# A light attention with a top-80 mixture of experts: one projection product per token group, earlier output clearing, and a listed order

## The chip, the cores and the metric

The kernel runs on one core of a Trainium2 chip. The metric is the device time of one execution in microseconds (us); lower is better. Of the kernel before there are three timed runs and one profiled execution.

## The reference

The input x has 8 x 3584 = 28672 tokens of 192 numbers, and each token has 8 heads with 7 raw weights. The first part replaces each token by a weighted sum over itself and the six tokens before it, with a softmax of the seven weights in each head:

```
w = exp(weight_gen - max);  w = w / (sum(w) + 1e-9)
out = einsum('bshk,bskhg->bshg', w, x_unf)
```

The second part is a mixture of 8 experts on the result. Each token goes to the expert of its largest gate logit; each expert keeps at most its 80 tokens of highest gate probability; every other row of the output is zero:

```
logits = x @ w_gate;  expert_idx = argmax(logits);  gate_w = softmax(logits)[expert_idx]
for e: keep = the (at most) 80 tokens of e with the largest gate_w
       out[keep] = gate_w[keep] * (relu(x[keep] @ w1[e]) @ w2[e])
```

So all tokens need logits, and only 640 rows need the experts and are stored with values other than zero.

## The kernel before, in words

**Stage A, logits of all tokens** (`gates`). The 128 partitions hold 128 runs of 224 consecutive tokens. x comes in 28 loads of 8 token positions (L385), transposed, from the host's layout: 96 partitions hold six of the eight positions, and the 32 further partitions hold the other two in three pieces, so a load is a full 128 x 1536 tile of 768 KB. TensorE projects each load on the gate, head by head, into a PSUM bank `pt`: four matmuls with 96 rows and 384 columns (L439) for the first six positions, then twelve with 32 rows and 128 columns (L444), three per output piece, for the other two. Only one `pt` bank exists. ScalarE copies it out (L448), TensorE transposes it into the PSUM tile `y` (L482), and for each of 14 chunks (8, 9, 9 and eleven times 18 positions) the seven-tap products with the softmax weights are formed head by head: five heads on VectorE, three on GpSimd (L547; in the last two chunks four on GpSimd, `NPOOL`). TensorE sums the products by transposing matmuls into `acc` (L563, seven per head), ScalarE copies, and TensorE turns the chunk back (`bt`, L577). The softmax of the raw weights runs three chunks ahead (L408 to L415), and `gate` turns the logits of a few chunks into gate probabilities.

**Stage B, selection.** For every expert a threshold is found: the top values per lane (`MAX` at L920), two rounds of counting (L871, L876), then the chosen tokens are numbered, their rows are gathered (L979), ranked exactly, and the totals are checked.

**Stage C, experts.** For the gathered rows the attention is done again in full (L992 to L1040, "attend"), then come the two matrix products of each expert (L1295 and L1299 up, L1319 down; "FFN"; expert 0 and 1 with 128 columns and the others with 80), and the scaled rows are stored to their places (L1334).

**Zeros of the output.** 28 transfers of 768 KB from a cleared tile `zt` (L1588) write the zeros. 22 go out during and after the loads of x; the last six (`late_zeros`) take a second tile `zt2` that is cleared only when the gathers have been issued.

**Order.** A `Plan` collects all operations with costs and dependences, and a list scheduler with random restarts (`order`) fixes the order on every engine. Each engine then issues in this order and waits by semaphores. Transfers of x, of the raw weights, of expert weights and zeros share SyncE's queue. Buffers: 4 of x (the same ring holds w1), 6 of raw weights (the same ring holds halves of w2). `issue` puts otherwise useless matmuls ("fillers") into TensorE's idle time: 128x128 ones before the first `acc` (`spin`, L643), 128x512 ones in stage B (L1325) and among the attends (L1268, L1269), and 14 before anything else (L637).

**Start.** The gate is loaded by three DMAs from ScalarE's queue (L338, L340), because the block layout `bd` is needed on 96 and on 32 partitions; VectorE takes the differences (L359) and fills `bd` (L362). GpSimd clears `zt`, `lg`, `vt` and some small tables by memsets.

Of the kernel before, what the change touches and what calls it, by code (L numbers as in the profile page):

```python
# [9 lines left out]
F32 = mybir.dt.float32  # L10
# [21 lines left out]
NQ = 1 + DH // (P - DH)  # L32
# [4 lines left out]
NPOOL = [3] * (len(SIZES) - 2) + [4] * 2  # L37
# [6 lines left out]
XB = 4  # L44
WB = 6
# [11 lines left out]
LATE = GE[-3]  # L57
NC = C
NH = 2
# [13 lines left out]
ZT = 512  # L73
# [3 lines left out]
SEED = 9  # L77
NOISE = (0.3, 1.0, 3.0, 6.0)
WE = 2
FILL = 0.6  # L80
FILL0 = 0.9
POOLED = frozenset(['am4', 'am5', 'bad', 'gs4', 'gs6', 'gx7', 'hb', 'hbt', 'kp0', 'lad', 'ohf0', 'pr00', 'pr10', 'pr11', 'pr21', 'pr61', 'pr70', 'prc1', 'sid', 'thr', 'v11'])
ZA = 18
ZH = 22
ZS = 10
ZP = 1.5
# [5 lines left out]
class Plan:  # L92
# [4 lines left out]
    READY = {"PE": 0.6, "ACT": 2.0, "DVE": 3.3, "POOL": 2.0}  # L97
    SAME = {"PE": 0.0, "ACT": 0.1, "DVE": 0.08, "POOL": 0.06, "DMA": 0.0}

    def __init__(self):  # L100
# [14 lines left out]
        self.port = []  # L115

# [54 lines left out]
    def _run(self, pred, succ, prio, rel, fwd):  # L171
# [19 lines left out]
        for _ in range(n):  # L191
# [13 lines left out]
            if best is None:  # L205
# [4 lines left out]
                    key=lambda k: (est[k] if fwd and e == "DMA" else 0.0, prio[k], k))  # L210
# [22 lines left out]

    def order(self):
        ops = self.ops
# [98 lines left out]

def consts(tc, cp, gate):
    nc = tc.nc
    gg = cp.tile([P, 2, NQ, E], F32, name="gg")
# [18 lines left out]
    for lo, hi, qa, qb in ((0, DH, NQ - 1, NQ), (DH, P, 0, NQ - 1)):
        for t in range(2):
            gt = gg[lo:hi, t, qa:qb]
# [9 lines left out]
def gates(pl, tc, pools, xt, wgen, ident, bd, epst, zb, lg, V, VL, tie, after, clear, ZH):  # L368
# [1347 lines left out]
```

## Time and profile before

| what | value |
|---|---|
| three runs | 257.09 us median (256.98 to 257.61) |
| profiled execution, own time | 257.11 us |
| its span, first to last instruction | 255.3 us |
| TensorE busy | 233.2 us, 91% of the span |
| VectorE busy | 187.5 us, 73% |
| GpSimd busy | 183.4 us, 72% |
| ScalarE busy | 87.4 us, 34% |
| moved by DMA | 68.36 MB, mean 268 GB/s |

The span leaves 1.8 us of the profiled time outside. A busy share is a mean over stages, so the sections below go by stretches of the span: up to 27 us the ramp, to 160 us the rest of stage A, to 196 us the selection with the first attends, and then the experts. A row of the timeline reads: start, duration, engine, line, operation, output and input, and in brackets how long the engine had been idle before and what ended that.

### The profile page before, as it was taken

How to read it: one execution, taken by the hardware profiler on the slowest of the kernel's cores; microseconds unless marked ns; L12 is line 12 of the kernel's file. 1: busy time of each engine (PE TensorE's matmuls, PEld its weight loads, DVE VectorE, ACT ScalarE, POOL GpSimd, SP SyncE). 2: the span in 40 equal slices, each digit the busy share in tenths (PEclk: the TensorE clock that was granted, in tenths of full speed). 3: DMA queues.
4: the chain of work that ended last, by engine and by line, in shares of the span. 5: the costliest groups of instructions: out<-in, count | busy, mean ns of one | idle time of the engine just before them, and what ended most of it. 6: DMA issues, size and time to landing. Idle time of an engine off the chain costs nothing. (4 is left out here: it accounts for less than half of the span.)

```text
span 255.3 us, 5886 instructions
## 1 busy us (share of the span) xinstructions
PE 233.2 (91%) x2317; PEld 184.1 (72%) x2317; DVE 187.5 (73%) x377; ACT 87.4 (34%) x215; POOL 183.4 (72%) x197
## 2 busy tenths in 40 slices
PE   8689999999999999999999999559789999999970
PEld 3457668788769878976888989347337897999960
DVE  2663679679949968999996999886583549899300
ACT  2341554283336227246613452320012122232310
POOL 6597688999979997998993979437477644436320
PEclk9955999999999999999999999755665799999997
DMA  6994778999969899859999996200899789995000
GB/s 231 425 349 154 274 242 233 361 307 407 341 200 416 334 287 384 337 188 278 412 400 406 401 383 263 62 0 17 202 347 385 238 296 289 332 283 197 19 13 17
DMA packets 22642, 68.36 MB, mean 268 GB/s; under 512 B 2418, under 2 KB 2935, under 8 KB 22608
## 3 DMA queue, kind: packets, MB, share of 16 engines
q1 hardware_dynamic: 20704, 63.05, 68.2%
q0 software_dynamic: 1472, 4.85, 7.6%
q8 instruction: 20, 0.33, 0.5%
q14 instruction: 14, 0.11, 0.1%
q10 hardware_dynamic: 432, 0.01, 0.1%
HBM read 45.40 MB, written 22.59 MB: 266 GB/s over the span
## 5 line engine op out<-in xcount | busy, mean ns | idle before, releaser
L563 PE MATMUL acc<-ident,P 128*126 128x128 f32 (+1 forms) x700 | 86.5, 278 | 0.0
L547 POOL TENSOR_TENSOR P<-ysb,w 128x882 f32<-128x882 f32 (+2 forms) x44 | 76.6, 1773 | 12.5 <-ACT ysb L502 12.4
L563 PEld LDWEIGHTS acc<-ident,P 128*126 128x126 f32 (+1 forms) x700 | 77.8, 141 | 5.2 <-issue 3.6
L547 DVE TENSOR_TENSOR P<-y,w 128x882 f32<-128x882 f32 (+2 forms) x68 | 61.9, 961 | 13.3 <-ACT hs L508 12.2
L444 PEld LDWEIGHTS pt<-x,bd 32*32 32x32 f32 x672 | 17.3, 108 | 21.0 <-issue 18.1
L448 ACT ACTIVATE yt<-pt 128x512 f32<-128x512 f32 (+2 forms) x29 | 16.8, 581 | 37.9 <-PE pt L444 37.8
L409 POOL TENSOR_TENSOR w<-w,m 128x1008 f32<-128x1008 f32 (+2 forms) x14 | 24.8, 1780 | 4.9 <-DVE m L408 4.9
L444 PE MATMUL pt<-x,bd 32*32 32x128 f32 x672 | 25.3, 282 | 2.5 <-ACT yt L448 2.5
L415 POOL TENSOR_TENSOR w<-w,r 128x1008 f32<-128x1008 f32 (+2 forms) x14 | 25.2, 1816 | 2.3 <-DVE gm L614 1.2
L439 PE MATMUL pt<-x,bd 96*32 96x384 f32 x224 | 25.2, 523 | 0.0
L1319 PE MATMUL F<-w,hu 128*80 128x192 f32 (+1 forms) x128 | 22.7, 326 | 0.0
L1023 DVE TENSOR_REDUCE ao<-pr 80x96 f32<-80x672 f32 (+3 forms) x14 | 18.0, 1305 | 4.0 <-POOL pr L1019 4.0
L1319 PEld LDWEIGHTS F<-w,hu 128*80 128x80 f32 (+1 forms) x128 | 18.7, 160 | 1.1
L412 DVE TENSOR_REDUCE m<-w 128x144 f32<-128x1008 f32 (+2 forms) x14 | 14.9, 1074 | 5.3 <-ACT w L411 5.3
L482 PE MATMUL y<-ident,yt 128*128 128x128 f32 (+1 forms) x116 | 17.6, 285 | 0.8 <-ACT yt L448 0.8
L411 ACT ACTIVATE w<-w 128x1008 f32<-128x1008 f32 (+2 forms) x14 | 13.3, 948 | 11.0 <-POOL w L409 11.0
L482 PEld LDWEIGHTS y<-ident,yt 128*128 128x128 f32 (+1 forms) x116 | 13.7, 146 | 2.6 <-issue 1.3
L408 DVE TENSOR_REDUCE m<-w 128x144 f32<-128x1008 f32 (+2 forms) x14 | 14.6, 1063 | 1.2 <-DMA w<-wgen 1.1
L414 DVE RECIPROCAL r<-m 128x144 f32<-128x144 f32 (+2 forms) x14 | 13.2, 947 | 2.3 <-ACT m L413 2.2
L1019 POOL TENSOR_TENSOR pr<-gx 88x672 f32<-88x672 f32 (+2 forms) x6 | 9.8, 1647 | 6.1 <-DVE gx L998 6.0
L1299 PE MATMUL F<-ax,w 128*128 128x80 f32 x96 | 13.7, 266 | 0.0
L1334 POOL DMA_INDIRECT out<-yo,sidx x6 | 6.2, 1042 | 10.0 <-ACT yo L1332 7.2
(268 smaller groups left out, 330.1 us busy)
## 6 DMA issues: line engine op xcount, KB each, us to landing
x<-xt SPq DMA_DIRECT2D x28, 768.0 KB, 6.0
out<-zt SPq DMA_DIRECT2D x28, 768.0 KB, 10.2
w<-w2p SPq DMA_DIRECT2D x16, 384.0 KB, 6.7
w<-w1p SPq DMA_DIRECT2D x8, 768.0 KB, 7.3
w<-wgen SPq DMA_DIRECT2D x11, 504.0 KB, 6.5
w<-wgen SPq DMA_DIRECT2D x2, 252.0 KB, 5.2
w<-wgen SPq DMA_DIRECT2D x1, 224.0 KB, 2.8
gx<-wgen,tux POOLq DMA_INDIRECT x6, 5.0
```

The lines of the kernel that those rows point to most:

```text
L408: op("DVE", dve(nw), lambda: nc.vector.tensor_reduce(out=m(), in_=w(), axis=AX.X, op=ALU.max), r=[wn], w=[mn])
L409: op("POOL", pool_flat(nw), lambda: nc.gpsimd.tensor_tensor(out=w(), in0=w(), in1=bcast_last(m(), K), op=ALU.subtract), r=[mn], w=[wn])
L412: op("DVE", dve(nw), lambda: nc.vector.tensor_reduce(out=m(), in_=w(), axis=AX.X, op=ALU.add), r=[wn], w=[mn])
L415: op("POOL", pool_flat(nw), lambda: nc.gpsimd.tensor_tensor(out=w(), in0=w(), in1=bcast_last(r(), K), op=ALU.mult), r=[rn], w=[wn])
L439: o = nc.tensor.matmul(pl[f"pt{g}"][32 * c:32 * c + 32, 0:3 * P], lhsT=bd[0:DH, c % 2, NQ - 1, :], rhs=x[0:DH, 3 * c:3 * c + 3, :], start= ...
L444: o = nc.tensor.matmul(pl[f"pt{g}"][32 * c:32 * c + 32, 3 * P:4 * P], lhsT=bd[DH:P, c % 2, r, :], rhs=x[DH:P, 3 * c + r, :], start=(r == 0 ...
L448: op("ACT", act(hi - lo), lambda: nc.scalar.activation(out=pl[f"yt{g}"][:, lo:hi], in_=pl[f"pt{g}"][:, lo:hi], func=AF.Copy), r=[f"pt{g}"] ...
L482: o = nc.tensor.matmul(pl[yn][:, u - s0 + sh:v - s0 + sh, :], lhsT=src, rhs=idn, is_transpose=True, start=True, stop=True)
L547: return (nc.gpsimd if onpool else nc.vector).tensor_tensor(out=out, in0=in0, in1=in1, op=ALU.mult)
L563: o = nc.tensor.matmul(pl[an][0:M, :], lhsT=pl[f"P{c}_{i}"][:, k, 0:M], rhs=ident, is_transpose=True, start=(n == 0 and k == 0), stop=(n = ...
L1023: V_(K * G * (h1 - h0), lambda h0=h0, h1=h1: v.tensor_reduce(out=pl[sn][0:rows, h0 * G:h1 * G], in_=pl[pn][0:rows, :, h0 * G:h1 * G].rearr ...
L1319: o = nc.tensor.matmul(yp(), lhsT=hs[q]()[:, j * n:(j + 1) * n], rhs=pl[f"w2_{e}{q}"][:, j % 2 * 2 + j // 2, :], start=(q == 0 and j == 0) ...
```

## The change

1. **x on 96 partitions.** The host now lays all eight positions on 96 partitions and pads 32 partitions with zeros: a load is a 128 x 2048 tile of 1 MiB, and the projection is four matmuls with 96 rows and 512 columns (L498 of the changed kernel). The twelve 32-row matmuls are gone. `bd`, the mask and the gate lie on 96 partitions, and the gate is one DMA.
2. **Clears on ScalarE.** A helper `blank` copies from a small zero tile by ScalarE activations (L397); 14 such clears stand before the first exponential on ScalarE. Three casts per group of selection candidates (`split`) move from GpSimd to ScalarE too.
3. **Zeros.** Rows of 3 KB in place of 2 KB; all 28 transfers from one tile, marked `spare`, so that the scheduler sends them when nothing else is due; no late zeros.
4. **Banks and fillers.** The small selection products no longer use the `pt` bank but parts of two `y` tiles (`S1`, `S2`). Fillers in stage B write to `S2` (`keep_awake`, L1331, L1332); the fillers of the ramp have 512 columns.
5. **Three heads on GpSimd in all chunks.**
6. **A listed order.** A table `STARTS` of one start per operation gives the order of every engine; the scheduler is used only if the table does not fit.

```diff
-NPOOL = [3] * (len(SIZES) - 2) + [4] * 2
+NPOOL = [3] * len(SIZES)
-ZT = 512
+ZT = 768
+STARTS = """
+7l 96 5k 63 l4 83 8l gw cf 73 ia al bq dg y0 yw m5 zs w3 xa 9l go h4 hw kp i3 bi b0 iz bw jp d3 mv vm wt 8d b5 g2 1o
...
-ZH = 22
-ZS = 10
-ZP = 1.5
+ZS = 5
+ZP = 0.8
...
+        return nc.scalar.activation(out=a, in_=z, func=AF.Copy)
+    pl.op("ACT", act(n), go, w=nm)
...
-    nc.scalar.dma_start(gg[0:DH, :, NQ - 1, :], gate.rearrange("(t d) e -> d t e", d=DH))
-    for t in range(2):
-        nc.scalar.dma_start(gg[DH:P, t, 0:NQ - 1, :], gate[t * DH:(t + 1) * DH].rearrange("(r d) e -> d r e", d=P - DH))
+    gg = cp.tile([DH, 2, E], F32, name="gg")
+    nc.scalar.dma_start(gg, gate.rearrange("(t d) e -> d t e", d=DH))
...
-        new(f"x{n}", lambda: xp.tile([P, 12, P], F32, name=f"x{n}", tag="x"), "x", XB)
+        new(f"x{n}", lambda: xp.tile([P, 16, P], F32, name=f"x{n}", tag="x"), "x", XB)
...
-            if lo == 0:
-                for c in range(4):
-                    o = nc.tensor.matmul(pl[f"pt{g}"][32 * c:32 * c + 32, 0:3 * P], lhsT=bd[0:DH, c % 2, NQ - 1, :],
-                                         rhs=x[0:DH, 3 * c:3 * c + 3, :], start=True, stop=True)
-            if hi == 4 * P:
-                for r in range(NQ - 1):
-                    for c in range(4):
-                        o = nc.tensor.matmul(pl[f"pt{g}"][32 * c:32 * c + 32, 3 * P:4 * P], lhsT=bd[DH:P, c % 2, r, :],
-                                             rhs=x[DH:P, 3 * c + r, :], start=(r == 0), stop=(r == NQ - 2))
+            for c in range(4):
+                o = nc.tensor.matmul(pl[f"pt{g}"][32 * c:32 * c + 32, lo:hi], lhsT=bd[:, c % 2, :],
+                                     rhs=x[0:DH, 4 * c + lo // P:4 * c + hi // P, :], start=True, stop=True)
...
-        for _ in range(int(gap * FILL0 / 0.1067)):
-            nc.tensor.matmul(pl["warm"][:, 0:P], lhsT=zb, rhs=zb, start=True, stop=True)
+        for _ in range(int(gap * FILL0 / 0.2134)):
+            nc.tensor.matmul(pl["warm"], lhsT=zb, rhs=with_ap(zb, [[0, 4], [1, P]]), start=True, stop=True)
...
-        op("POOL", pool(n), lambda: g.tensor_copy(out=p(2), in_=c()), r=[f"cand{nm}"], w=[f"pv{nm}"])
+        op("ACT", act(n), lambda: nc.scalar.activation(out=p(2), in_=c(), func=AF.Copy), r=[f"cand{nm}"], w=[f"pv{nm}"])
...
-        bank(bn, [RC, 2])
+        bsv = lambda: pl["S1"][0:RC, 0, 2 * E + 2 * q:2 * E + 2 * q + 2]
...
-    def late_zeros():
-        op("POOL", pool(8), lambda: nc.gpsimd.memset(zt2[:, 0:8], 0.0), w=["zt2b"], dep=[sm["go"]])
-        for _ in range(ZH, NZ):
-            clear(late=True)
...
+    def keep_awake():
+        new("S2", lambda: ps_y.tile([P, 3, 512], F32, name="S2", tag="y"), "y", 2, parts=["warmy", "plc", "tfp"])
+        def fill(gap):
+            for _ in range(int(gap * FILLY / 0.2134)):
+                nc.tensor.matmul(pl["S2"][:, 0, :], lhsT=zb, rhs=with_ap(zb, [[0, 4], [1, P]]), start=True, stop=True)
...
-        def zero(i, eng=nc.sync, src=zt):
-            return eng.dma_start(ov[:, i * ZC:(i + 1) * ZC].rearrange("p (a b) -> p a b", b=ZT),
-                                 with_ap(src, [[0, ZC // ZT], [1, ZT]]))
+        def zero(i):
+            return nc.sync.dma_start(ov[:, i * ZC:(i + 1) * ZC].rearrange("p (a b) -> p a b", b=ZT),
+                                     with_ap(zt, [[0, ZC // ZT], [1, ZT]]))
...
+                    pl.spare.add(zeros[-1])
...
-    xt = np.empty((NX_, P, 2, 2, 3, P), dtype=x.dtype)
+    xt = np.zeros((NX_, P, 2, 2, 4, P), dtype=x.dtype)
```

**TensorE in the middle of stage A.** `pt` are projections, `acc` the sums of a chunk's products (seven matmuls per head), `y` the transposes. Before:

```order
L439 MATMUL pt_994<-x_809,bd 32x384 x4
L444 MATMUL pt_994<-x_809,bd 32x128 x12
L563 MATMUL acc_925<-ident,P_3_933 126x128 x7
L563 MATMUL acc_925<-ident,P_4_949 126x128 x7
L439 MATMUL pt_1040<-x_838,bd 32x384 x4
L444 MATMUL pt_1040<-x_838,bd 32x128 x12
L563 MATMUL acc_1064<-ident,P_0_1013 126x128 x7
```

In the changed kernel:

```order
L617 MATMUL acc_770<-ident,P_3_762 126x128 x7
L617 MATMUL acc_770<-ident,P_4_780 126x128 x7
L498 MATMUL pt_862<-x_718,bd 32x512 x4
L617 MATMUL acc_872<-ident,P_0_815 126x128 x7
L617 MATMUL acc_872<-ident,P_5_833 126x128 x7
L498 MATMUL pt_896<-x_740,bd 32x512 x4
```

Each projection is one group of four matmuls in place of two groups of four and twelve; what stands between two projections is the same kind of work.

**VectorE around the last product of stage A.** `P_..<-y` are products, `cand` the top eight of an expert's lanes, `ix` their places, `gm` belongs to the gate probabilities. Before:

```order
L920 MAX cand<-vt 112x8 x6
L547 TENSOR_TENSOR P_3_2348<-y_2119,w_1402 128x882
L920 MAX cand<-vt 112x8
L928 MAX_INDEX ix<-cand,vt 112x8 x6
L610 TENSOR_REDUCE gm_2391<-lg 128x18
```

In the changed kernel, from the last product on:

```order
L601 TENSOR_TENSOR P_4_1971<-y_1699,w_1193 128x882
...
L974 MAX cand<-vt 112x8
L669 RECIPROCAL gm_1939<-gm_1939 128x18
L974 MAX cand<-vt 112x8
L672 SCALAR_TENSOR_TENSOR VL<-lg,gm_1939 128x144
L974 MAX cand<-vt 112x8 x3
L982 MAX_INDEX ix<-cand,vt 112x8
L974 MAX cand<-vt 112x8
L982 MAX_INDEX ix<-cand,vt 112x8
L974 MAX cand<-vt 112x8
```

All eight `MAX` now stand behind the last product; before, seven of them stood ahead of it.

**SyncE at the end of the loads of x.** `x` are loads, `out<-zt` zeros, `w_<n>` from `w1p` and `w2p` expert weights. Before:

```order
L385 DMA x_1847<-xt 128x1536
L1588 DMA out<-zt 128x3x512
L1252 DMA w_0_1916<-w1p 128x1536
L1588 DMA out<-zt 128x3x512 x10
L1259 DMA w_10_2292<-w2p 128x768
...
L1588 DMA out<-zt_65 128x3x512 x6
L1252 DMA w_4_2875<-w1p 128x1536
```

In the changed kernel:

```order
L445 DMA x_1557<-xt 128x2048
L1303 DMA w_0_1588<-w1p 128x1536
L1310 DMA w_10_1619<-w2p 128x768
L1303 DMA w_1_1632<-w1p 128x1536
L1303 DMA w_2_1661<-w1p 128x1536
L1651 DMA out<-zt 128x2x768 x3
L1310 DMA w_11_1775<-w2p 128x768
...
L1651 DMA out<-zt 128x2x768 x10
L1303 DMA w_4_2510<-w1p 128x1536
```

Eight zeros stand ahead of the last load of x where eleven did, and the other 20 stand behind it, between the weights of the first four experts, ahead of the fifth expert's.

## Rows read from the trace of the kernel before

**Rows 1.** Page, busy time and share of the span, by engine.

```profile
PE 233.2 (91%) x2317; PEld 184.1 (72%) x2317; DVE 187.5 (73%) x377; ACT 87.4 (34%) x215; POOL 183.4 (72%) x197
```

**Rows 2.** Windows: length, busy time (instructions) per engine, PEclk, DMA share, GB/s.

```profile
27.00:160.00 133.00, 132.96 (x1615) 107.47 (x1612) 116.48 (x162) 59.83 (x131) 120.57 (x89) 1.00 0.90 325
160.00:196.00 36.00, 26.82 (x181) 16.91 (x180) 25.00 (x121) 6.40 (x25) 19.76 (x42) 0.59 0.52 161
...
0.00:120.00 120.00, 115.67 (x1374) 85.52 (x1375) 91.75 (x119) 50.89 (x102) 104.17 (x100) 0.94 0.85 301
124.00:140.00 16.00, 15.96 (x178) 13.57 (x177) 13.94 (x17) 4.99 (x15) 12.42 (x10) 1.00 1.04 406
12.00:27.00 15.00, 14.24 (x121) 9.14 (x119) 7.62 (x14) 4.86 (x12) 11.14 (x19) 0.54 0.73 270
```

**Rows 3.** Timeline of TensorE's matmuls, 30 to 33 us.

```profile
30.04 0.85 PE L439 MATMUL pt<-x,bd 96*32 96x384 f32 x8
30.82 0.86 PE L444 MATMUL pt<-x,bd 32*32 32x128 f32 x24
31.61 1.64 PE L563 MATMUL acc<-ident,P 128*126 128x128 f32 x13
```

**Rows 4.** Instruction groups by shape: busy us, mean ns, idle before and releaser.

```profile
L547 POOL TENSOR_TENSOR P<-ysb,w 128x882 f32<-128x882 f32 x35 | 67.5, 1962 | 9.2 <-ACT ysb L502 9.0
L547 DVE TENSOR_TENSOR P<-y,w 128x882 f32<-128x882 f32 x53 | 54.0, 1065 | 5.1 <-ACT hs L508 4.7 <-PE acc L563 0.2
L444 PE MATMUL pt<-x,bd 32*32 32x128 f32 x672 | 25.3, 282 | 2.5 <-ACT yt L448 2.5
```

**Rows 5.** Timeline of all engines, first 10 us.

```profile
3.83 0.16 DVE L359 TENSOR_TENSOR gg<-gg 96x7 f32<-96x7 f32 x1 [2.57 <-DMA gg<-gate]
...
6.79 0.17 DVE L359 TENSOR_TENSOR gg<-gg 32x21 f32<-32x21 f32 x1 [0.32 <-DMA gg<-gate]
...
8.11 0.97 POOL L409 TENSOR_TENSOR w<-w,m 128x448 f32<-128x448 f32 x1 [3.42 <-DVE m L408]
...
9.11 0.58 ACT L411 ACTIVATE w<-w 128x448 f32<-128x448 f32 x1 [5.61 <-POOL w L409]
```

**Rows 6.** Timeline of TensorE's matmuls in the ramp.

```profile
12.87 1.51 PE L439 MATMUL pt<-x,bd 96*32 96x384 f32 x8
14.31 1.50 PE L444 MATMUL pt<-x,bd 32*32 32x128 f32 x24
...
19.11 1.51 PE L439 MATMUL pt<-x,bd 96*32 96x384 f32 x8
...
21.99 3.24 PE L563 MATMUL acc<-ident,P 128*112 128x128 f32 x14
```

**Rows 7.** Waits of SyncE's queue: releaser, us in total, times, longest.

```profile
SPq L385 <- PE pt L444: 71.6, 23, 5.8
```

**Rows 8.** Timeline of TensorE, end of stage A.

```profile
146.54 0.85 PE L439 MATMUL pt<-x,bd 96*32 96x384 f32 x8
...
158.80 1.69 PE L563 MATMUL acc<-ident,P 128*126 128x128 f32 x14
```

**Rows 9.** Timeline of VectorE, selection and first attends.

```profile
154.37 1.30 DVE L920 MAX8 cand<-vt 112x8 f32<-112x136 f32 x6
...
184.02 0.21 DVE L992 TENSOR_REDUCE amc<-gxc 80x8 f32<-80x56 f32 x1 [1.17 <-DMA gxc<-wgen,idc]
```

**Rows 10.** Timeline of TensorE, experts 0 to 2.

```profile
196.56 1.06 PE L1295 MATMUL F<-at3b,w 128*128 128x256 f32 x2
...
201.97 1.47 PE L1319 MATMUL F<-w,hu 128*128 128x192 f32 x8
...
205.74 0.60 PE L1295 MATMUL F<-at3b,w 128*128 128x256 f32 x2
...
209.25 2.77 PE L1319 MATMUL F<-w,hu 128*128 128x192 f32 x16
...
213.80 0.43 PE L1295 MATMUL F<-axb,w 128*128 128x160 f32 x2
```

More of the change, by code (lines that the diff above doesn't have):

```diff
@@ L209, in _run @@
                      and (not port[k] or held_until[3 - port[k]] <= t + 1e-9)),
-                    key=lambda k: (est[k] if fwd and e == "DMA" else 0.0, prio[k], k))
+                    key=lambda k: (est[k] + 1e4 * (k in self.spare) if fwd and e == "DMA" else 0.0, prio[k], k))
             ready[e].remove(i)
@@ L232, in _run, with given @@
         return start
+    def given(self):
+        ops = self.ops
+        t = [int(x, 36) / 100.0 for x in STARTS.split()]
+        if len(t) != len(ops):
+            return None
+        place = {i: n for n, i in enumerate(sorted(range(len(t)), key=lambda i: (t[i], i)))}
+        if any(place[p] > place[i] for i, o in enumerate(ops) for p in o[3] | o[6]):
+            return None
+        self.start = t
+        return sorted(place, key=place.get)
     def order(self):
+        got = self.given()
+        if got is not None:
+            return got
         ops = self.ops
@@ L660, in gates @@
                 yg += 1
-                while nz < min(ZA, ZH) and yg + XB - 1 >= ZS + nz * ZP:
+                while nz < NZ and yg + XB - 1 >= ZS + nz * ZP:
                     clear([xs[yg + XB - 1]])
@@ L781, in tables, with selection @@
     return t
-def selection(pl, tc, pools, zb, V, VL, tie, ident, t, cap, wgen, xw, xh, w1, w2, out, flag, clear, zt2):
+def selection(pl, tc, pools, zb, V, VL, tie, ident, t, cap, wgen, xw, xh, w1, w2, out, flag):
     nc = tc.nc
@@ L921, in early @@
                    [f"vt1{e // 4}", f"cs{e}"], [f"cand{a}"])
-        new("S1", lambda: ps_y.tile([P, 3, 512], F32, name="S1", tag="y"), "y", 2, parts=["S1a", "S1b"])
         threshold()
+        new("S1", lambda: ps_y.tile([P, 3, 512], F32, name="S1", tag="y"), "y", 2, parts=["S1a", "S1b0", "S1b4"])
         for a, b in GR:
@@ L1243, in check @@
         bads = scratch("bads", [P, 1], BF16)
-        V_(2 * E + 7, lambda: v.tensor_reduce(out=bads, in_=bad, axis=AX.X, op=ALU.max), ["bad"], ["bads"])
+        V_(2 * E + 2 * NH + 3, lambda: v.tensor_reduce(out=bads, in_=bad, axis=AX.X, op=ALU.max), ["bad"], ["bads"])
         bank("fp", [P, 1])
@@ L1271, in keep_warm @@
         pl.fillers.append(([wi], [], fill))
-    ys = ["S1"] + [f"y{c}" for c in range(len(CHUNKS))]
+    ys = [f"y{c}" for c in range(len(CHUNKS))] + ["S1", "S2"]
+    def keep_awake():
[3 more added lines that the diff above has]
+                nc.tensor.matmul(pl["S2"][:, 0, :], lhsT=zb, rhs=with_ap(zb, [[0, 4], [1, P]]), start=True, stop=True)
+        wi = op("PE", 0.22, lambda: nc.tensor.matmul(pl["S2"][:, 0, :], lhsT=zb, rhs=with_ap(zb, [[0, 4], [1, P]]), start=True,
+                                                     stop=True), r=["zb"], w=["warmy"])
+        stop = []
+        pl.fillers.append(([wi], stop, fill))
+        return stop
     def late_banks():
@@ L1688 @@
             for t in range(2):
-                for i in range(3):
+                for i in range(4):
                     xt[n, :DH, q, t, i] = xd[t, :, (8 * n - HALO + 2 * i + q) % L]
-                    xt[n, DH:, q, t, i] = xd[t, 32 * i:32 * i + 32, (8 * n - HALO + 6 + q) % L]
     w1 = np.asarray(inputs["moe_w1"])
```

184 lines of the change are left out of this document (112 added, 72 removed).

## The prediction

> **What bounds the kernel now.** I start with the busy shares of the page: TensorE 91%, VectorE 73%, GpSimd 72% [rows 1]. A mean over stages does not say which of the three can be relieved, so I read the windows next [rows 2]. From 27 to 160 us TensorE is busy 132.96 of 133.00 us at a granted clock of 1.00, that is 2.4 GHz: this stretch is bound by TensorE alone. But VectorE has 116.48 and GpSimd 120.57 us of work in it, so either is next as soon as TensorE gets 12 to 16 us lighter. From 12 to 27 us the granted clock is 0.54, nearly all of it the lower level of 1.2 GHz, and TensorE is busy 14.24 of 15.00 us: the ramp is TensorE at half speed. From 160 to 196 us no engine is full and the clock is 0.59: a chain of short steps. Last come the waits of SyncE's queue: 23 of its loads of x wait 71.6 us in all for a projection to free a buffer [rows 7]. So the loads follow TensorE, and not TensorE the loads.
>
> **Part 1, the projection, in the steady stretch.** The timeline shows what one load of x costs TensorE at full clock: the 96-row products start at 30.04, the 32-row ones at 30.82 and the next work at 31.61, so 0.78 + 0.79 = 1.57 us [rows 3]. In the changed kernel the first part has 512 columns for 384. In proportion that is 0.78 x 512/384 = 1.04 us, and the second part is gone: 0.53 us less per load. 672 of the 32-row products in groups of 24 records are 28 loads [rows 4]; three or so lie ahead of 27 us, so 25 remain: 25 x 0.53 = 13.3 us. TensorE's work falls from 133.0 to 119.7 us.
>
> The trace runs the two groups one behind the other, 0.78 and then 0.79 us [rows 3]. By the Trainium skill, page *TensorEngine Tiling (Array Packing)*, section Key Properties, tiles of the array work independently and different tiles can execute in parallel; if the small products had run beside the large ones, removing them would save nothing and this term would be 0 in place of the 7.5 taken below. By that rule, the trace disagrees.
>
> Not all of the 13.3 us comes through. Three heads on GpSimd in the last two chunks in place of four move two products: VectorE + 2 x 1.07 = 118.6 us, GpSimd - 2 x 1.96 = 116.6 us [rows 2, 4]. Seven of the eight `MAX` go out of the stretch (6 in 1.30 us, so 0.22 each, 1.5 in all [rows 9]): VectorE 117.1 us. Three engines with 117 to 120 us each, that hand on to one another through two `y` tiles and a few product buffers, do not all run without gaps. If TensorE still had none, VectorE would be busy 117.1/119.7 = 98%; in the stretch before it is 116.48/133 = 88%. I take the middle, 93%: 117.1/0.93 = 125.9, so about **-7.5 us** (133 to 125.5). Ends: 0 (the gain is lost to gaps) and -13.3.
>
> **Part 2, the ramp.** One gate load for three: VectorE's first difference ran at 3.83 and its last, held by the gate's later loads, at 6.79 [rows 5]. All of `bd` hangs on the first load now, so the first `max` and GpSimd's subtraction (8.11 before [rows 5]) may move up by up to 2.9 us. Against that stand 14 clears on ScalarE ahead of the first exponential, which began at 9.11 after 5.61 us of idle time [rows 5]. The clears are bounded by that row: an activation of 448 columns took 0.58 us, so the two large ones (768 and 1088 columns) cost 1 to 1.4 us, three middling ones 0.3 to 0.4 and the rest about 0.2, together some 4 to 5 us in those 5.61 idle. They cover up to about 7.5 us, where the subtraction would allow 6.2. I count -1.6 us at the first exponential (7.5 against 9.11).
>
> Behind it the clock decides. Two projections lie ahead of the first `acc`, at 12.87 and 19.11, each 2.88 us at the low clock (12.87, 14.31, then 1.44 more), and `acc` starts at 21.99 [rows 6]. With the clock up and the new shape they take 1.04 each: -3.7 us. The fillers there have four times as many columns each now, and less idle time stands between them, since the first copy out of `pt` comes earlier; so I expect that the clock stays up. After 21.99 the first 14 sums took 3.24 us [rows 6]; at full clock 13 such took 1.64 [rows 3]. That is 1.5 more, if the products are there. Against these -6.8 us stands that a load of x has a third more bytes, and the second and third load land later. I take **-6**. Ends: -1.5 (the clock falls as before) and -8.
>
> **Part 3, selection.** The seven `MAX` that stood ahead of the last product stand behind it, in the chain to the threshold: 7 x 0.22 = **+1.5** [rows 9]. Own banks for the small products and the casts on ScalarE shorten some hops; no row prices that, so the ends are 0 and +2.5.
>
> **Part 4, first attends.** VectorE waited 1.17 us for gathered rows at 184.02 [rows 9]; that step now stands behind the ranking work, and with no zeros in flight the rows should come earlier: -1.2. The transposes of the attends ran at 0.5 clock; with heavier fillers in the 36 us at 0.59 [rows 2] I count 0.8 more, **-2** in all, ends 0 and -3.
>
> **Part 5, experts.** The up products of expert 0 took 201.97 - 196.56 = 5.4 us, those of expert 1, with the same shapes at full clock, 209.25 - 205.74 = 3.5 [rows 10]: -1.9 if the clock is up. Sixteen down products of expert 1 start at 209.25 and last 2.77, and expert 2 starts only at 213.80 [rows 10]: 1.8 to 2 us in which fillers wait for attend 2, which now stands ahead of that. **-4** together, ends 0 and -4.5. The rest of the experts, the same products in the same number, is counted at nothing.
>
> Zeros, their rows of 3 KB and the clears otherwise are counted at nothing, covered by a queue that waited 71.6 us for buffers [rows 7]; what it costs if that cover is gone is the rival on transfers.
>
> **Sum.** -7.5 - 6 + 1.5 - 2 - 4 = -18.0 us against the profiled execution's own 257.11: 239.1, and I write 239.0. (The median of the runs is 257.09, so nothing is to be added for that.) The ends of the terms that hang together: all low -28, all high about 0; neither is likely as a whole.
>
> **Rivals.**
> - *Gaps eat the projection's gain.* VectorE stays at 88% of its time in the steady stretch, as before [rows 2]: 117.1/0.88 = 133, so no gain there. All else as forecast: 239 + 7.5 = 246.5. For it: VectorE idled for ScalarE's `y` copies in the stretch while TensorE was the bound [rows 4]. Against it: a TensorE that is full makes others wait, and these waits go with it. 0.15.
> - *The clock stays at 1.2 GHz* in the ramp and up to expert 0. Then the ramp gives 1.5 to 2, expert 0 nothing, the attends 1.2: 239 + 4 + 1.9 + 0.8 = 245.7. For it: the clock fell to 0.54 though fillers ran. 0.12.
> - *Transfers become the bound, mildly.* Up to the last load of x the changed queue has 28 x 1.049 (x) + 6.4 (raw weights) + 8 x 0.786 (zeros) + 0.8 = 42.9 MB, against 37.9 before. At 301 GB/s, the mean of the first 120 us [rows 2], the last x lands at 142.5. From the last projection to the end of the last sum it was 146.54 to 160.5, 14 us [rows 8], so stage A would end at 156.5 and the gains of parts 1 and 2 together are 4 in place of 13.5: 248.5. 0.06.
> - *Transfers become the bound, severely, and the kernel is slower.* Same mechanism, same place. The later parts give 4.5 us, so the kernel is slower than before if stage A ends after 165, that is if the last x lands after 151: below 42.9 MB / 151 us = 284 GB/s. The mean over the whole span was 268: then the last x lands at 160 + some latency, stage A ends near 175, and the time is about 257 + 15 - 4.5 = 267.5. Against it: 406 GB/s at a full share from 124 to 140 us [rows 2], where zeros were written without a break. 0.05.
>
> There are 63 MB ahead of the fifth expert's weights in the changed queue; at 406 GB/s they end by 156 us, at 325 by 194. By the Trainium skill, page *DMA: Bandwidth & Descriptors*, section on bandwidth in its specifications, traffic between HBM and SBUF is bound at about 358 GB/s per core; an estimate from this page is 177 us for these 63 MB and 120 us for the 42.9 MB up to the last x, late for the zeros and not for x. The trace shows more than that limit, 406 GB/s, for 16 us.
>
> **How the numbers follow.** The forecast's case, all parts near their terms, has 0.62 and lies between 231 and 244.5. Gaps (246.5) 0.15, clock (245.7) 0.12, mild transfers (248.5) 0.06, severe ones (267.5) 0.05. The range of **231 to 250** holds the first four but the tails. All but the last case are faster by more than 0.3% (0.8 us, about what a measurement here can tell from no change); 0.02 of the mixtures may fall within it: faster 0.92, same 0.02, slower 0.06.
>
> **What would show it.** Right: projections about 1.04 us apart from the next work; a first `acc` near 16 us with a granted clock near 1 in the ramp; VectorE and GpSimd above 90% busy in the steady stretch, and its end near 147; a clock near 1 at the first product of expert 0; no gap ahead of expert 2. Wrong: a projection that takes the full 1.57 us; a clock near 0.5 ahead of the first `acc`; TensorE waiting for x in the steady stretch, with the DMA share near 1 throughout; a selection longer by more than the 1.5 us.

## The result, and the profile after

| | before | changed |
|---|---|---|
| runs | 256.98, 257.09, 257.61, 738.63 us | 240.14, 241.91, 242.22, 243.02 us |
| median | 257.35 us | **242.06 us** |
| profiled execution, own time (span) | 257.11 (255.3) us | 240.14 (238.4) us |

The ratio of the runs is 0.940, with a 95% interval from 0.933 to 0.947. Medians and ranges here take in every execution, while ratios leave out disturbed ones, such as the one at 738.63 us (in experiments 6 and 9 to 12 they are half or more of one side). The forecast was 239.0 us, its range 231 to 250. The profiled execution of the change, 17.0 us below that of before, is the fastest of the four; a likely reason why the others are up to 2.9 us slower is given below (experiments 10 and 12). The points of time given for the changed kernel are from it, so the stages add up to more than the 15.3 us between the medians.

The windows of the changed kernel, columns as in [rows 2]:

```profile
12.00:27.00 15.00, 14.55 (x107) 7.76 (x107) 13.06 (x21) 9.27 (x20) 14.63 (x19) 1.00 1.02 417
27.00:140.00 113.00, 108.95 (x936) 85.54 (x933) 103.04 (x120) 52.01 (x114) 106.52 (x60) 1.00 0.99 387
140.00:160.00 20.00, 10.97 (x71) 7.65 (x70) 17.60 (x85) 8.20 (x32) 4.16 (x13) 0.75 1.01 397
160.00:196.00 36.00, 30.48 (x228) 22.74 (x228) 24.02 (x89) 5.98 (x22) 24.81 (x31) 0.85 0.64 183
```

Against [rows 2] the ramp has the clock up (1.00 for 0.54) and all of TensorE, VectorE and GpSimd busy in it. From 27 to 140 us TensorE is no longer full alone: it is 96% busy, GpSimd 94%, VectorE 91%. The transfers run at a share of 0.99, and still the loads wait for buffers, as before [rows 7]:

```profile
SPq L445 <- PE pt L498: 62.5, 24, 5.3
```

One projection now, from TensorE's timeline of the changed kernel, the answer to [rows 3]: it starts at 13.01 and the next work at 14.01, 1.00 us where it was 1.57, at full clock already in the ramp; the first sums start at 17.39, where they started at 21.99 [rows 6].

```profile
13.01 1.06 PE L498 MATMUL pt<-x,bd 96*32 96x512 f32 x8
14.01 0.82 PE L697 MATMUL warm<-zb 128*128 128x512 bf16 x3
...
16.35 1.07 PE L498 MATMUL pt<-x,bd 96*32 96x512 f32 x8
17.39 1.83 PE L617 MATMUL acc<-ident,P 128*112 128x128 f32 x14
```

The start, all engines, answers to [rows 5]. The gate arrives once; the subtraction begins at 4.87 in place of 8.11, is done by 5.84, and the exponential starts only at 7.00, behind the last clear:

```profile
3.68 0.17 DVE L419 TENSOR_TENSOR gg<-gg 96x14 f32<-96x14 f32 x1 [2.63 <-DMA gg<-gate]
...
4.87 0.97 POOL L469 TENSOR_TENSOR w<-w,m 128x448 f32<-128x448 f32 x1 [1.16 <-DVE ev L788]
...
6.87 0.22 ACT L397 ACTIVATE bad<-zb 128x23 f32<-128x23 bf16 x1
7.00 0.56 ACT L471 ACTIVATE w<-w 128x448 f32<-128x448 f32 x1
```

For the stages I use the copy of each chunk's sums by ScalarE (L569 before, L623 after), which starts when a chunk is through TensorE, and a few points of the timelines:

| point, us | before | changed | moved by |
|---|---|---|---|
| sums of the first chunk | 29.82 | 22.72 | -7.1 |
| of the third | 42.97 | 34.64 | -8.3 |
| of the twelfth | 143.55 | 125.48 | -18.1 |
| of the last (fourteenth) | 160.58 | 144.19 | -16.4 |
| last turn back (L577, L631) | 160.89 | 145.39 | -15.5 |
| first step of the exact ranking (L1151, L1202) | 178.16 | 166.43 | -11.7 |
| first product of expert 0 | 196.56 | 181.53 | -15.0 |
| first product of expert 2 | 213.80 | 197.11 | -16.7 |
| end of the span | 255.3 | 238.4 | -16.9 |

### The profile page after: what moved, and what is told of

It is laid out like the page before. It is cut to its first block, busy times and chain, and to the rows that moved or that the text cites. A ratio compares the mean times of both kernels' runs of the same rounds, so it can differ in the third digit from the quotient of the medians.

```text
span 238.4 us, 4530 instructions
## 1 busy us (share of the span) xinstructions
PE 209.8 (88%) x1635; PEld 160.2 (67%) x1635; DVE 187.5 (79%) x374; ACT 93.4 (39%) x241; POOL 172.4 (72%) x167
## 5 line engine op out<-in xcount | busy, mean ns | idle before, releaser
L617 PEld LDWEIGHTS acc<-ident,P 128*126 128x126 f32 (+1 forms) x700 | 76.5, 140 | 21.0 <-issue 7.8
L617 PE MATMUL acc<-ident,P 128*126 128x128 f32 (+1 forms) x700 | 85.1, 275 | 2.5 <-DVE P L601 1.7
L601 POOL TENSOR_TENSOR P<-ysb,w 128x882 f32<-128x882 f32 (+2 forms) x42 | 73.8, 1779 | 3.0 <-ACT ysb L556 2.9
L601 DVE TENSOR_TENSOR P<-y,w 128x882 f32<-128x882 f32 (+2 forms) x70 | 63.7, 961 | 7.1 <-ACT hs L562 5.3
L498 PE MATMUL pt<-x,bd 96*32 96x512 f32 (+2 forms) x232 | 30.0, 590 | 1.1 <-ACT lg L634 1.1
L502 ACT ACTIVATE yt<-pt 128x512 f32<-128x512 f32 (+2 forms) x29 | 16.8, 578 | 21.4 <-PE pt L498 21.2
L1079 DVE TENSOR_REDUCE ao<-pr 80x96 f32<-80x672 f32 (+3 forms) x14 | 18.1, 1310 | 3.6 <-POOL pr L1075 3.6
L472 DVE TENSOR_REDUCE m<-w 128x144 f32<-128x1008 f32 (+2 forms) x14 | 15.1, 1080 | 5.2 <-ACT w L471 5.2
L1399 POOL DMA_INDIRECT out<-yo,sidx x6 | 6.0, 1008 | 17.3 <-DMA out<-yo,sidx 4.2
L536 PEld LDWEIGHTS y<-ident,yt 128*128 128x128 f32 (+1 forms) x116 | 12.9, 141 | 7.2 <-issue 4.5
L536 PE MATMUL y<-ident,yt 128*128 128x128 f32 (+1 forms) x116 | 16.4, 276 | 1.5 <-ACT yt L507 1.2
L1364 PEld LDWEIGHTS F<-ax,w 128*128 128x128 f32 x96 | 13.2, 191 | 0.0
L556 ACT ACTIVATE ysb<-y 128x504 f32<-128x504 f32 (+2 forms) x14 | 8.1, 579 | 10.8 <-PE y L536 10.8
L1360 PE MATMUL F<-axb,w 128*128 128x160 f32 x48 | 11.2, 315 | 0.0
```

What stands on the lines that cost most here:

```text
L472: op("DVE", dve(nw), lambda: nc.vector.tensor_reduce(out=m(), in_=w(), axis=AX.X, op=ALU.add), r=[wn], w=[mn])
L498: o = nc.tensor.matmul(pl[f"pt{g}"][32 * c:32 * c + 32, lo:hi], lhsT=bd[:, c % 2, :], rhs=x[0:DH, 4 * c + lo // P:4 * c + hi // P, :], sta ...
L502: op("ACT", act(hi - lo), lambda: nc.scalar.activation(out=pl[f"yt{g}"][:, lo:hi], in_=pl[f"pt{g}"][:, lo:hi], func=AF.Copy), r=[f"pt{g}"] ...
L536: o = nc.tensor.matmul(pl[yn][:, u - s0 + sh:v - s0 + sh, :], lhsT=src, rhs=idn, is_transpose=True, start=True, stop=True)
L601: return (nc.gpsimd if onpool else nc.vector).tensor_tensor(out=out, in0=in0, in1=in1, op=ALU.mult)
L617: o = nc.tensor.matmul(pl[an][0:M, :], lhsT=pl[f"P{c}_{i}"][:, k, 0:M], rhs=ident, is_transpose=True, start=(n == 0 and k == 0), stop=(n = ...
```

## The experiments

Every median is over all executions of a kernel. The kernel before, run beside each group, had medians of 257.05 (experiments 1 to 4), 256.89 (5 to 8), 257.49 (9 to 11) and 255.49 us (12). The changed kernel was not run again in these groups; comparisons with it are with its 242.06 us above.

**1. The projection undone.** Layout of x, bd and gate as before; everything else stays.

```diff
-                o = nc.tensor.matmul(pl[f"pt{g}"][32 * c:32 * c + 32, lo:hi], lhsT=bd[:, c % 2, :],
...
+                    o = nc.tensor.matmul(pl[f"pt{g}"][32 * c:32 * c + 32, 0:3 * P], lhsT=bd[0:DH, c % 2, NQ - 1, :],
...
+                        o = nc.tensor.matmul(pl[f"pt{g}"][32 * c:32 * c + 32, 3 * P:4 * P], lhsT=bd[DH:P, c % 2, r, :],
...
```

> The changed kernel with the projection, its layout of x and the three gate loads as before (four products of 384 columns and twelve of 32 rows per load); listed order, clears, fillers and zeros stay changed. Theory (TensorE bounds the middle of stage A, the projection gives the gain there): the projection costs 1.57 us again, the tenth chunk's sums end 8 to 11 us later than in the changed kernel, time 250 to 254 us. Rival (the listed order gives the gain, the projection is beside other work): at most 3 us later, 242 to 245.

Measured: 255.13 us (254.06 to 257.57), ratio to before 0.999 [0.994, 1.005]: nothing of the gain is left. Its sums of the first chunk come at 26.93, those of the tenth at 118.12, 15.1 later than in the changed kernel (103.01), those of the eleventh 17.4 later (132.38 for 115.03), and the last at 160.54, as before. Its window shows why: TensorE is full again.

```profile
27.00:140.00 113.00, 112.56 (x1418) 88.31 (x1411) 90.95 (x98) 49.65 (x105) 97.02 (x55) 1.00 0.85 289
```

The theory holds, and the size was more than expected (15.1 us for 8 to 11 at the tenth chunk, of which 4.2 come from the ramp and its three gate loads): a ramp that was 2.9 us ahead of the kernel before at the first chunk brought nothing at the last. The two groups of a projection run one behind the other here too (0.79 us each).

**2. The projection alone.** The kernel before with the new layout, the four products and the one gate load; scheduler (with cost estimates for the new load and product), clears, fillers and zeros of before.

```diff
...
+                o = nc.tensor.matmul(pl[f"pt{g}"][32 * c:32 * c + 32, lo:hi], lhsT=bd[:, c % 2, :],
+                                     rhs=x[0:DH, 4 * c + lo // P:4 * c + hi // P, :], start=True, stop=True)
...
```

> The kernel before with the new projection alone: x on 96 partitions, four products of 512 columns, one gate load; order by the scheduler, clears on GpSimd, old zeros and fillers. Theory: 6 to 12 us faster than before (245 to 251), the clock in the ramp still near 0.5. Rival (without the new order nothing comes through): 255 to 258. If loads of a third more bytes bind under the old order of zeros: slower than 258.

Measured: 244.96 us (243.94 to 246.44), ratio 0.957 [0.950, 0.964]: 12.1 of the 15.3 us, at the fast end of what was expected. Sums of the first chunk at 21.85, of the twelfth at 125.44: the same as in the changed kernel to 0.9 us. Against the expectation, the granted clock is 1.00 in the ramp with the old fillers:

```profile
12.00:27.00 15.00, 12.28 (x104) 7.77 (x104) 12.43 (x21) 8.89 (x20) 13.95 (x14) 1.00 1.01 416
```

What it lacks lies behind stage A: from the last sums to expert 0 it takes 40.0 us, the changed kernel 37.3.

**3. The list taken away.** `STARTS = ""`, so the scheduler finds the order.

> The changed kernel with an empty table of starts, so that the scheduler finds the order. Theory (the order is worth little beside the projection, the ramp's clock and the first attends): 240 to 246 us. Rival (the listed order carries the gain): over 250.

Measured: 243.72 us (241.94 to 255.66), ratio 0.948 [0.940, 0.957], whose interval overlaps that of the changed kernel. The theory holds. Stage A is as short (last sums 142.43); from there to expert 0 it takes 40.5 us, and most of the loss lies behind the first step of the ranking (17.9 us from it to expert 0, for 15.1). The listed order may be worth some 1.7 us, in the first attends; the intervals do not separate it from nothing.

**4. Clears on GpSimd.**

```diff
-        return nc.scalar.activation(out=a, in_=z, func=AF.Copy)
-    pl.op("ACT", act(n), go, w=nm)
+        return nc.gpsimd.memset(a, 0.0)
+    pl.op("POOL", pool(n), go, w=nm)
```

> The changed kernel with the 14 clears as memsets on GpSimd at the same places of the listed order. Theory (the clears were hidden on either engine): within 1 us of the changed kernel, 241 to 243. Rival (GpSimd, which is over 95% busy from 12 to 27 us, is late with the first subtraction): the first chunk's sums end 2 to 3 us later, and the time is 243.5 to 245.

Measured: 243.86 us (241.03 to 244.92), ratio 0.945 [0.937, 0.954]. Sums of the first chunk 0.8 us later than in the changed kernel (23.51), and still 0.8 at the twelfth (126.25). The sums fit the theory and the time the rival's range: on ScalarE the clears are worth 0.8 us in the ramp, and the rest of the time is within the runs' spread.

**5. Three gate loads.** `bd` on 128 partitions as before, though only 96 are read.

> The changed kernel with the gate loaded by three transfers and the block layout formed on 128 partitions as before; the projection reads only the 96 partitions. Theory (the last gate load held VectorE's first maximum 2.9 us): the first maximum goes from 4.2 back to about 7 us, first sums 2 to 3 us later, time 243.5 to 246. Rival (the load of x and ScalarE's clears hold the ramp anyway): first sums within 1 us, time 240 to 243.

Measured: 245.22 us (244.53 to 246.21), ratio 0.955 [0.950, 0.961]. Sums 2.7 us later at the first chunk (25.42) and 2.7 at the twelfth (128.21). The theory holds. In its ramp TensorE waits 3.0 us for the first copy out of `pt`, and the clock is 0.79 from 12 to 20 us; the kernel before had such a wait at the same place. The row of experiment 5, then that of before; in the changed kernel this product starts at 8.81 without a wait:

```profile
11.11 0.85 PE L505 MATMUL pt<-x,bd 96*32 96x384 f32 x8 [3.01 <-ACT yt L509]
```

```profile
11.15 0.86 PE L444 MATMUL pt<-x,bd 32*32 32x128 f32 x24 [2.54 <-ACT yt L448]
```

**6. No fillers in the ramp.** `FILL0 = 0.0`.

> The changed kernel without the useless matmuls of the ramp (FILL0 = 0; the 14 at the very start stay). Theory of the prediction (the heavier fillers keep the clock up in the ramp): granted clock near 0.5 in a part of the stretch from 12 to 27 us, first chunk's sums 3 us later or more, time 244 to 247 us. Rival (the chain is short enough now that the clock stays up without them): clock 1.00, sums within 1 us, time as the changed kernel, 240 to 243.

Measured: 246.42 us (242.81 to 247.06; the profiled one 246.78), ratio 0.951 [0.943, 0.959]. In the profiled one the clock is low, and sums come 2.7 us later at the first chunk (25.44) and at the twelfth (128.19):

```profile
12.00:20.00 8.00, 6.74 (x28) 2.64 (x29) 5.49 (x10) 4.86 (x10) 7.31 (x13) 0.50 1.01 417
```

So the changed kernel's fillers hold its clock, as the theory said; that it takes 512-column ones is not so, since the clock stays up with the old ones in experiment 2.

**7. No fillers in the selection.** `FILLY = 0.0`.

> The changed kernel without the fillers that write to S2 between the selection's products (FILLY = 0). Theory (they bring the clock up ahead of the first attends and of expert 0): from the ranking to the first product of expert 0 about 2 us longer, that expert's up products 5 us in place of 3.6, time 243.5 to 246. Rival (the clock rises by the useful work): 240 to 243.

Measured: 244.13 us (243.04 to 245.05), ratio 0.948 [0.944, 0.953]. From the last sums to expert 0 39.7 us for 37.3, and the first three quarters of that expert's up products run at half speed. TensorE's timeline, then the changed kernel's:

```profile
186.82 1.06 PE L1360 MATMUL F<-at3b,w 128*128 128x256 f32 x2
...
192.74 1.50 PE L1384 MATMUL F<-w,hu 128*128 128x192 f32 x8
```

```profile
181.53 0.59 PE L1360 MATMUL F<-at3b,w 128*128 128x256 f32 x2
...
185.26 1.50 PE L1384 MATMUL F<-w,hu 128*128 128x192 f32 x8
```

The theory holds in the trace: 5.9 us where the changed kernel takes 3.7, and from the first step of the ranking to expert 0 17.7 us for 15.1. (In the total 2.1 us are seen of it, and the intervals overlap: with everything later, the wait for gathered rows ahead of expert 2 is gone.)

**8. The second relu first.** In the changed kernel expert 1's down products wait for VectorE, and VectorE for rows; three rows of VectorE, then two of TensorE:

```profile
194.60 0.21 DVE L1048 TENSOR_REDUCE am<-gx 80x8 f32<-80x56 f32 x1 [2.62 <-DMA gx<-wgen,tux]
194.84 0.21 DVE L1049 TENSOR_TENSOR gx<-gx,am 80x56 f32<-80x56 f32 x1
194.97 0.68 DVE L1378 TENSOR_SCALAR hu<-F 128x512 f32<-128x512 f32 x1
```

```profile
195.71 1.57 PE L1384 MATMUL F<-w,hu 128*128 128x192 f32 x8 [1.68 <-DVE hu L1378]
197.11 0.43 PE L1360 MATMUL F<-axb,w 128*128 128x160 f32 x2
```

One entry of the table (operation 922) is altered:

```diff
-        t = [int(x, 36) / 100.0 for x in STARTS.split()]
+        t = [int(x, 36) / 100.0 for x in STARTS.split()]; t[922] = min(t[922], 178.22)
```

> The changed kernel with one entry of the table altered: VectorE takes expert 1's second relu (L1378) ahead of the two steps of attend 3 that wait for gathered rows. Theory (the wait of 2.62 us for these rows holds expert 1's down products by 1.68 us, and so all that follows): expert 2 starts 1.5 to 2 us sooner after expert 0, time 1.5 us less than the changed kernel. Rival (the next attend, delayed by nothing, is still late, or the gap opens at a later expert): no change, within 0.5 us.

Measured: 241.67 us (239.65 to 244.11), ratio 0.938 [0.933, 0.943]. Expert 2 starts at 195.06, 13.4 us after expert 0 where it was 15.6, as the theory had it; but its second group of products waits, and expert 3 starts 0.7 us sooner than in the changed kernel (202.00 for 202.69): most of the gain is given back.

```profile
195.06 0.43 PE L1360 MATMUL F<-axb,w 128*128 128x160 f32 x2
196.14 0.67 PE L1364 MATMUL F<-ax,w 128*128 128x80 f32 x4 [0.64 <-ACT ax L1096]
```

The wait went to ScalarE, where the copy of `ax` (195.87) stands behind an exponential (195.71) of the next attend's rows, which VectorE had got at 195.18. The rival holds in the main: the median is 0.4 us below the changed kernel's.

**9. The load on 96 partitions.** The padding is not loaded.

```diff
-        xs[i] = op("DMA", XCOST if i else XFIRST, lambda: nc.sync.dma_start(pl[f"x{n}"], xt[n]), w=[f"x{n}"])
+        xs[i] = op("DMA", XCOST if i else XFIRST, lambda: nc.sync.dma_start(pl[f"x{n}"][0:DH], xt[n][0:DH]), w=[f"x{n}"])
```

> The changed kernel with the 96 partitions of x that the projection reads loaded, and not the 32 of padding: 768 KB for 1 MiB per load, 7.3 MB less in all. Theory (transfers are hidden behind TensorE, VectorE and GpSimd): sums of each chunk within 0.5 us of the changed kernel, time the same, 240 to 243.5 us. Rival (at a DMA share of 0.99 the padding costs time): 2 us or more faster, 240 or less in the median. If a load on 96 partitions is slower than one on 128: slower.

Measured: median 259.43 us (253.16 to 266.58), ratio 1.000 [0.992, 1.008]: with a quarter less of x to load the whole gain is gone; neither theory nor rival holds, but the last condition of the expectation. In the profiled execution (261.92), at the same share of the DMA engines, they move 266 GB/s in place of 417 in the ramp, a load lands after 15.0 us in the median (9.3 in the changed kernel), and TensorE waits for x. The window of the ramp and a row of the waits:

```profile
12.00:27.00 15.00, 13.64 (x99) 7.68 (x99) 12.88 (x21) 9.29 (x20) 14.64 (x19) 1.00 1.03 266
```

```profile
PE pt L498 <- DMA x<-xt: 14.6, 9, 4.8
```

So without the padding the change gains nothing: the transfers bind, as in the prediction's rivals on transfers. The Trainium skill, page *SBUF — State Buffer*, section Door 1: The DMA port swizzle, says that a transfer's bandwidth goes with how many of the 16 ports its partitions reach, and the page's summary asks for 128 partitions. The trace agrees with that advice, with 417 and 266 GB/s. By the port table of that section 96 partitions reach all 16 ports too, so their number does not explain the loss, and no run here shows what does.

**10. The addition of epsilon on ScalarE.** The four executions of the changed kernel differ by up to 2.9 us. Up to the twelfth chunk the sums come at the same time to 0.04 us in the profiles of the changed kernel and of experiments 7 and 8; the thirteenth's come at 134.87, 138.15 and 134.85. In between VectorE has one short step, two instructions of L668; the row of the changed kernel, then that of experiment 7:

```profile
126.33 0.27 DVE L668 TENSOR_SCALAR gm<-gm 128x36 f32<-128x36 f32 x2
```

```profile
126.35 2.13 DVE L668 TENSOR_SCALAR gm<-gm 128x36 f32<-128x36 f32 x2
```

In experiment 7 the step ends as GpSimd's product does (122.25 + 6.18 = 128.43, and the next VectorE work starts at 128.39); in the changed kernel it lies where one of GpSimd's three products ends and the next begins. TensorE then waits 1.74 us in the changed kernel and 3.59 in experiment 7, and after the longer wait the clock falls (0.83 from 130 to 140 us, where the changed kernel has 1.00). Its rows, and the window of experiment 7:

```profile
127.73 0.95 PE L617 MATMUL acc<-ident,P 128*126 128x128 f32 x7 [1.74 <-DVE P L601]
```

```profile
129.60 1.22 PE L617 MATMUL acc<-ident,P 128*126 128x128 f32 x7 [3.59 <-DVE P L601]
```

```profile
130.00:140.00 10.00, 9.49 (x73) 9.28 (x71) 8.11 (x15) 3.05 (x9) 4.90 (x5) 0.83 0.84 318
```

None of the three slower executions of the changed kernel was profiled, so that this step makes them slower is likely and not shown; their mean granted clock, 0.933 to 0.935 where the fastest has 0.951, fits.

The edit, for the larger gates (the smaller keep the old step):

```diff
-        mv(f"gp{i}", n, lambda v: v.tensor_scalar(out=g(), in0=g(), scalar1=EPS, scalar2=None, op0=ALU.add), [], [gn])
+        if n > NC:
+            op("ACT", act(n), lambda: nc.scalar.activation(out=g(), in_=g(), func=AF.Identity, bias=epst[:, 0:1]), w=[gn])
+        else:
+            mv(f"gp{i}", n, lambda v: v.tensor_scalar(out=g(), in0=g(), scalar1=EPS, scalar2=None, op0=ALU.add), [], [gn])
```

> The changed kernel with one small step of the gates, the addition of epsilon (L668), on ScalarE in place of VectorE for the five larger gates. Theory (in some executions this step waits on VectorE until a long product of GpSimd is over, TensorE then stands idle 3.6 us in place of 1.7 and its clock falls, which makes the spread from 240 to 244 us): all or nearly all executions between 239 and 241 us, the chunk before the last has its sums near 134.9 us as in the fastest execution. Rival (the spread comes from elsewhere): executions between 240 and 244 us as before.

Measured: 243.56 us (242.64 to 246.54), ratio 0.947 [0.942, 0.952]. The step is gone from VectorE, and its neighbours lose more: the two products for V (L672, there L675) take 4.65 us for 3.36, the two subtractions (L665) 4.35 for 2.52, and the twelfth chunk is 5 us late already (130.53).

```profile
117.67 4.65 DVE L675 SCALAR_TENSOR_TENSOR V<-lg,gm 128x352 f32<-128x352 f32 x2
...
124.08 4.35 DVE L665 TENSOR_TENSOR lg<-lg,gm 128x288 f32<-128x288 f32 x2
```

The cure failed: no execution of it is as fast as the changed kernel's median. The profiled one, at 246.54, is the slowest of the seven; but experiment 11, which has the same edit, was profiled in the fastest of its six, and there the two subtractions take 4.34 us and the twelfth chunk comes at 130.52, so this is not a matter of one slow execution. That these steps wait for GpSimd is what the ends of the rows suggest; it was not shown by taking the wait away.

**11. Two index steps later as well.** Experiments 8 and 10, and operations 874 and 868 (L1255, L1021) behind the product for the attends.

> The step on ScalarE as above, expert 1's second relu ahead of attend 3's wait, and two small index steps of VectorE (L1255, L1021) behind the product that feeds the first attends' transposes, since the first of them took 2.14 us until GpSimd's product was over. Theory: 1 to 2 us less than the step alone, 237.5 to 239.5 us. Rival (each gain is given back at the next attend): as the step alone, 239 to 241.

Measured: 243.58 us (242.87 to 244.73), ratio 0.949 [0.944, 0.954]: no gain over experiment 10, as the rival had it, though both lie above the times expected. In the changed kernel L1255 took 2.14 us; here it takes 0.15, but the product that now stands ahead of it takes 2.95 us for 0.84. The long step of the changed kernel ends as GpSimd's product does (178.39 and 178.37), and the long product here ends 0.7 us, about its usual time, behind GpSimd's (182.76 and 182.04). The row of the changed kernel, then those of experiment 11:

```profile
176.25 2.14 DVE L1255 SCALAR_TENSOR_TENSOR tix<-tx 80x6 f32<-80x6 f32 x1
```

```profile
179.81 2.95 DVE L1078 TENSOR_TENSOR pr<-gx 88x672 f32<-88x672 f32 x1
182.68 0.15 DVE L1258 SCALAR_TENSOR_TENSOR tix<-tx 80x6 f32<-80x6 f32 x1
```

**12. Fillers in the gap.** The second relu first, and 30 useless products into the sums' bank just before the thirteenth chunk's first sum.

```diff
+            if i == self.touch["acc12"][0]: self.gap()
...
+    pl.gap = lambda: [nc.tensor.matmul(pl["acc12"], lhsT=zb, rhs=zb, start=True, stop=True) for _ in range(30)]
```

> The changed kernel with expert 1's second relu ahead of attend 3's wait, and 30 useless 128-column products on TensorE just ahead of the first sum of the chunk before the last, where TensorE stood idle 1.7 us in the fast executions and 3.6 in the others. Theory (the spread from 240 to 244 us is this idle time, 1.9 us, and the clock that falls after the longer one, some 2 us): the clock stays at 1.00 from 130 to 140 us in every execution and at most the 1.9 us of waiting is left: all executions between 239.5 and 242, median 240 to 241.5. Rival (the clock does not hang on this gap, or products in the gap delay the sums): 241.5 to 244 us as without them.

Measured: six executions from 241.69 to 242.27, median 242.03; ratio 0.959 [0.955, 0.964], which is to executions of before of 251.41 to 253.22 us, faster than in any other group, and can't be set beside the other ratios. The profiled execution has the long VectorE step (2.12 us), and the clock stays up all the same; the thirteenth's sums come at 136.70, between the 134.87 and 138.15 above:

```profile
125.81 1.84 PE L699 MATMUL acc<-zb 128*128 128x128 bf16 x30
129.47 0.98 PE L618 MATMUL acc<-ident,P 128*126 128x128 f32 x7 [1.83 <-DVE P L602]
```

```profile
130.00:140.00 10.00, 9.05 (x82) 8.63 (x81) 9.21 (x20) 3.21 (x10) 4.90 (x5) 1.00 0.87 326
```

So between these profiles the fallen clock is worth 1.45 us and the longer wait 1.85. The theory's mechanism holds, and the six lie within 0.6 us; but all lie in the rival's range of times, and the median is that of the changed kernel: no version here beats it clearly.

## Why the prediction was right

The direction, the place and the range held; the time came out 3.1 us above the forecast, 1.1 in the profiled execution. That it came so near is in part luck: in the profiled execution stage A and the first attends gave 4.2 us more than forecast, the selection (from the last sums) and the experts 5.5 less. One of the prediction's own signs of being wrong came, a selection longer by more than 1.5 us.

- *Part 1, steady stretch, -7.5.* A projection costs 1.00 us where 1.04 was taken. (The prediction's own quotient, 125.9 us, gives -7.1 and not -7.5.) From the third to the twelfth chunk the time went from 100.6 to 90.8 us, -9.7, but the last two chunks gave back 1.7; with the ramp the last sums come 16.4 us sooner, where the two parts had 13.5. VectorE came out at 91% busy to 140 us, between the 88 and 98 that the middle was taken from. If tiles that can run in parallel (the Trainium skill, *TensorEngine Tiling (Array Packing)*, section Key Properties) had done so here, the term would have been nothing. Experiment 1 shows that the two groups, whose tiles differ in shape and which write to one bank, do not; it does not test the rule for other tiles.
- *Part 2, ramp, -6.* -7.1 at the first chunk, -8.3 at the third. The first exponential starts at 7.00, where 7.5 was counted. Two pieces were tried and carry 2.7 us each: the one gate load and the fillers (5, 6); without either the clock falls in part of the ramp. Of the two reasons that the prediction gave for the clock, the larger fillers were not needed: with the old ones it stays up too (2). The other, less idle time since the first copy out of `pt` comes earlier, is what the rows show: the clock fell behind a wait for that copy before (2.54 us) and in experiment 5 (3.01 us).
- *Part 3, selection, +1.5.* This is the term that was mis-sized most: from the last turn back to the first step of the ranking it is 21.0 us for 17.3, **+3.8**. Most of the loss, 3.2 us, arises ahead of the first round of counting (L871, L925). That round started 0.6 us ahead of the last turn back and now starts 2.6 behind it (rows of VectorE, before and changed):

```profile
160.32 1.07 DVE L871 TENSOR_TENSOR gec<-cand,thr 112x896 bf16<-112x896 f32 x1
```

```profile
147.98 1.07 DVE L925 TENSOR_TENSOR gec<-cand,thr 112x896 bf16<-112x896 f32 x1
```

  In those 2.6 us VectorE works without a pause at three of the `MAX`, four of the eight index searches (L982, 0.4 us each) and a step of the gates. The seven `MAX` were counted; the searches, which before were done while TensorE still worked on the last chunk, were not. It is no effect of the listed order alone: with only the projection changed (2) the same stretch takes 21.2 us. The fillers do not hold the clock there either (0.75 from 140 to 160 us).
- *Part 4, first attends, -2.* From there to expert 0 15.1 us for 18.4, -3.3, with VectorE's wait for rows gone and the clock up by then; the fillers carry 2.6 of it (7).
- *Part 5, experts, -4.* From expert 0 to expert 2 15.6 us for 17.2, **-1.7**. The up products of expert 0 gave their 1.9 (3.7 us for 5.4). The gap ahead of expert 2 did not go: attend 2 was moved out of it, and a wait of 1.68 us for a relu that stands behind attend 3's rows came into it. The step by which the gap goes since attend 2 "now stands ahead of that" asked what is removed and not what is queued behind the next wait; experiment 8 shows that the next engine gives it back once more.
- *Rivals.* Mild and severe transfers did not come, at 388 GB/s in the first 120 us; experiment 9, at 266 GB/s in the ramp, shows how they would have. Gaps did not eat the projection's gain, with VectorE at 91% for 88. The low clock did not come in the ramp and for expert 0, but in the selection. The 2 to 3 us between executions were in no rival.

Experiments 1 and 2 show the cause: the projection, with its one gate load, makes 12.1 us alone, and without it the rest makes nothing. The gate load is the smaller piece, some 3 us of the total (5).

## What to carry to other kernels

When one engine is full over a long stretch, price the work that its next rivals hold in the same stretch: the gain ends where they do, what they did unseen beside the full engine comes out behind it (here the index searches), and moving small steps about before that engine is relieved bought nothing here. Padding can be cheaper than packing, in matmuls and in transfers, as it was here. And ask of every moved step not only which wait it leaves, but what stands behind the next one on each engine that serves it in order.

## What the runs showed of the hardware

With loads of x on 96 partitions the DMA engines moved 266 GB/s in the ramp where with loads on 128 they moved 417, at the same share of the engines; leaving out the zeros made the loads land 5.7 us later in the median (9).

Single steps of VectorE that take 0.15 us elsewhere lasted 2.1 us beside a product of GpSimd (L1255), and the same step can be short or long: the two instructions of L668 start at 126.31 in experiments 8 and 12 and take 0.27 us in the one and 2.12 in the other. L601 on VectorE, which reads `y` from PSUM, runs beside GpSimd's products at 1.06 us each in the mean. The Trainium skill, *SBUF — State Buffer*, section Who interferes with whom, says that the two share a pair of ports as a lock held for a whole instruction, which VectorE needs for two inputs from SBUF and for some single-input modes; the forms that stretched here (L668, L672, L665, L1255 and, in experiment 11, L1075, there L1078) fit, and the products from PSUM that did not stretch fit too. No run took the lock away by itself.

The granted clock fell to the lower level after waits of TensorE of 2.2 us (1), 2.5 (before), 3.0 (5) and 3.6 (7), and not after waits of 1.2 to 1.8 us in the same places; after a wait of 2.4 us in the twelfth chunk it fell in experiment 11 and not in 10.
